# A fused attention, soft-MoE and feed-forward kernel on one core: the combine softmax divided between the routing tail and the output stage, and the weight conversions cut into finer steps

## The chip, the cores and the metric

The kernel runs on 1 core of one Trainium2 chip. The metric is device time in microseconds; lower is better. In the text PE is TensorE, DVE is VectorE, ACT is ScalarE, POOL is GpSimd and SP is SyncE, which here only issues DMAs. Each engine works through a queue of its own, in order, and waits on semaphores for the others.

## The reference

Three layers follow each other. All inputs are float32.

```python
# attention, q k v: (8, 8, 576, 64), causal in blocks of 64
scores = scale * q @ k.T ; scores[block_i < block_j] = -1e9
x = softmax(scores) @ v                      # reshaped to (4608, 512)
# soft mixture of experts: 8 experts with 4 slots each
logits = x @ phi                             # (4608, 32)
d = exp(logits - logits.max(0)); d /= d.sum(0) + 1e-9      # over the tokens
slot_input = (d.T @ x).reshape(8, 4, 512)
slot_out[e] = relu(slot_input[e] @ w1[e]) @ w2[e]          # 512 -> 1024 -> 512
c = exp(logits - logits.max(1)); c /= c.sum(1) + 1e-9      # over the slots: combine
x = c @ slot_out.reshape(32, 512)
# feed forward, 512 -> 2048 -> 512
r = relu(x @ w_in); g = s * (r * r) + b
out = g @ w_out
```

## The kernel before

**Attention and routing** (0 to 433 us). 32 pairs of heads pass through a hand-written schedule: the table `SLOT` gives each step an offset, `at` puts it into `plan`, and `run` issues all steps sorted by time. The order of code here is the order in every engine's queue. After each fourth pair one batch is routed: its tokens are transposed and copied (xT), multiplied by phi (L469, L482), the running maximum `nrun` over tokens is updated (L473, L485), the exponentials are transposed (d, L509) and the weighted sum of tokens is added to `acc` (route_x, L511 to L527). `route_n` copies the logits to `lgs` (L532). After the last batch `route_w` (L540 to L544) makes W4, the weights that bring the four groups of partial sums together.

**Weights.** w1 and w2 of the experts come in 32 loads of 1 MB (w1 and w2, index 0 to 15 each), every load being two DMAs of 512 KB (load_w, L101). The 8 `wi` and 8 `wo` loads of the feed-forward layer hold 64-bit words, which are turned into float32 on chip by `from_f64`: two passes on DVE (cve L619, cvm L620), two on ACT (L622, L623), two on DVE (cvf L625, cve L626). Then a `wi` gets one multiplication (L739). A `wo` gets a multiplication (value, L702), a sum of absolute values and from it a power of two (power: ACT L706, DVE L709, ACT L711) and is split into two float16 halves (high: ACT L719, low: DVE L724). `from_f64` is a generator: a `yield` ends a step, and `convert` advances every active conversion by one step. Twelve loads come in during attention. The rest need a place: NPOST places of 1 MB, freed by `used` when an expert is done with its weights, and half of the place pairs of `wi` and `wo` that are through with conversion. SP issues all loads in a fixed order (advance, L684).

**The tail of routing** (L594 to L604). Thirteen `convert` calls are put into the plan, 0.8 of a schedule unit apart, so conversions of wi_0 to wi_3 go between the steps of the last batch's routing.

**The expert stage.** slotT, the slots' inputs, is made (L777, L778). Then `expert1` runs over the 16 w1 loads, all adding into one PSUM tile hp; `mid` (L828) evicts hp (hs), transposes it and applies relu (hTz); `expert2` runs over the 16 w2 loads into so. After each expert one `convert` follows, with at most two conversions active. Six generators `combine` (groups of six token tiles each) do the combine softmax and take a free slot among the active conversions: maximum (DVE), subtraction (POOL), exponential (ACT), sum and reciprocal (DVE), product (POOL), and the split into two float16 halves (ACT, POOL).

**The slots stage.** so is evicted (sos, L890), transposed, and multiplied by the eight converted `wi`; the result is scaled into mst (L887 to L939).

**The output stage.** 12 groups of three token tiles by 16 blocks of the hidden dimension give 192 steps: h (PE, L982), r (ACT, L984), g (DVE, L990), rh (ACT, L996), rl (DVE, L998), and nine matmuls into three output tiles (L1010 to L1012), which are issued LAG = 4 steps later. `ctrans` transposes the combine weights of the next group halfway through each.

Of the kernel before, what the change touches and what calls it, by code (L numbers as in the profile page):

```python
# [8 lines left out]
F32 = mybir.dt.float32  # L9
F32R = mybir.dt.float32r  # L10
F16 = mybir.dt.float16
# [3 lines left out]
AF = mybir.ActivationFunctionType  # L15
# [2 lines left out]
PSUM = bass.MemoryType.PSUM  # L18

NPRE = 12  # L20
NPOST = 4

SLOT = {
    "ld_k": -28.8, "ld_q": -28.6, "ld_v": -18.0,
# [8 lines left out]
}  # L33

# [6 lines left out]
def fused_kernel(  # L41
# [218 lines left out]
    def lo(eng, o, i, h):  # L260
        eng = {"P": POOL, "D": DVE}.get(eng, eng)
        eng.tensor_tensor(out=o, in0=i, in1=h, op=ALU.subtract)  # L262
# [285 lines left out]
    def at(tau, pri, fn, *args):  # L548
        plan.setdefault(tau, []).append((pri, len(plan[tau]) if tau in plan else 0, fn, args))
# [61 lines left out]
    def from_f64(w, pool, finish):  # L611

        v = w.rearrange("p (n t) -> p n t", t=2)
        l32, h32 = v[:, :, 0].bitcast(U32), v[:, :, 1]
        n = w.shape[1] // 2
        m = pool.tile([128, n], I32, tag="cvm", name="cvm", bufs=1)
        e = pool.tile([128, n], I32, tag="cve", name="cve")
        f = pool.tile([128, n], F32, tag="cvf", name="cvf")
        DVE.tensor_scalar(out=e, in0=h32, scalar1=1, scalar2=21, op0=ALU.logical_shift_left, op1=ALU.logical_shift_right)  # L619
        DVE.tensor_scalar(out=m, in0=h32, scalar1=0xFFFFF, scalar2=None, op0=ALU.bitwise_and)  # L620

        ACT.activation(out=f, in_=l32, func=AF.Copy, scale=2.0 ** -52, bias=1.0)  # L622
        ACT.activation(out=e, in_=e, func=AF.Relu, bias=m896, scale=2.0 ** 23)  # L623
        yield
        DVE.scalar_tensor_tensor(out=f, in0=m, scalar=2.0 ** -20, in1=f, op0=ALU.mult, op1=ALU.add)  # L625
        DVE.scalar_tensor_tensor(out=e, in0=h32, scalar=-0x80000000, in1=e, op0=ALU.bitwise_and, op1=ALU.bitwise_or)  # L626
        for fn in finish:
            fn(f, e.bitcast(F32))
            yield
# [22 lines left out]
    def later(stack, name, bufs, side="left"):  # L652
        return stack.enter_context(tc.tile_pool(name=name, bufs=bufs, side=side, reuse_waits="tile"))

    P = {}
    wlate = wholes(ctx, "wlate", 16 - NPRE, reuse_waits="tile")
    e1 = later(ctx, "e1", 1)
    P["cv"] = later(ph2, "cv", 2)
    wpost = places(ph2, "wpost", NPOST, reuse_waits="tile")
    ready, todo, active = set(), [], []  # L660
# [36 lines left out]
    def split_wo(i):  # L697
# [6 lines left out]
        def power(u, s):  # L704
            for h in range(2):
                ACT.activation(out=s[:, 512 * h:512 * h + 512], in_=u[:, 512 * h:512 * h + 512], func=AF.Abs, bias=eps,  # L706
                               accum_out=wsum[:, 2 * i + h:2 * i + h + 1])

            DVE.tensor_scalar(out=wpow[:, 2 * i:2 * i + 2].bitcast(I32), in0=wsum[:, 2 * i:2 * i + 2].bitcast(I32),  # L709
                              scalar1=0x7F800000, scalar2=0x7F800000, op0=ALU.bitwise_and, op1=ALU.bitwise_xor)  # L710
            ACT.mul(wpow[:, 2 * i:2 * i + 2], wpow[:, 2 * i:2 * i + 2], 2.0 ** 13)  # L711
# [17 lines left out]
                empty.append(split(home["wo", i], i))  # L729
                advance()  # L730

        return from_f64(wt["wo", i], P["cv"], [value, power, high, low])

    def conv_in(i):

# [11 lines left out]
    def convert(most):  # L747

        pump(active)
        if todo and len(active) < most and todo[0] in wt:  # L750
            key = todo.pop(0)
            active.append((conv_in if key[0] == "wi" else split_wo)(key[1]))

    T = dict(pe=1, g=0.447, r=1.648)

    CSUB = 1
    CMOST = 2
    with tc.manual_schedule():
        advance()
    todo += [key for key in wseq if key[0] in ("wi", "wo")]  # L760
    for i in range(13):
        at(TEND + 0.8 * i, 20, convert, 1)
    run(TEND, 1000)
    rt.close()
    P["cs"] = later(ctx, "csp", 1, "right").tile([128, NT, 64], F16, name="cs")
    e2 = later(ctx, "e2", 2, "right")
    P["hTz"] = later(ph2, "hp2", 1, "right").tile([128, 8, 288], F32, name="hTz")
    POOL.memset(P["hTz"], 0.0)
    pa = ph2.enter_context(tc.tile_pool(name="pa", bufs=1, space=PSUM, reuse_waits="tile"))
    pb = ph2.enter_context(tc.tile_pool(name="pb", bufs=2, space=PSUM, reuse_waits="tile"))  # L770
    with tc.manual_schedule():
# [11 lines left out]
        hp = pa.tile([128, 512], F32, name="hp")  # L783
        so = pa.tile([128, 512], F32, name="so")
        hs = e1.tile([128, 512], F32, tag="a1", name="hs")

        def combine(T, n):

            lg = lgs[:, T:T + n, :]
            mc = e2.tile([128, 6, 1], F32, tag="mc", name="mc")  # L790
            DVE.tensor_reduce(out=mc[:, :, 0], in_=lg, axis=AX, op=ALU.max)
            c = e2.tile([128, 6, 32], F32, tag="c", name="c")
            POOL.tensor_tensor(out=c, in0=lg, in1=mc.to_broadcast([128, n, 32]), op=ALU.subtract)
            yield
            ACT.activation(out=c, in_=c, func=AF.Exp)
            yield
            sc = e2.tile([128, 6, 1], F32, tag="sc", name="sc")
            DVE.tensor_reduce(out=sc[:, :, 0], in_=c, axis=AX, op=ALU.add)
            DVE.tensor_scalar(out=sc, in0=sc, scalar1=1e-9, scalar2=2.0 ** -14, op0=ALU.add, op1=ALU.mult)
            DVE.reciprocal(out=sc, in_=sc)  # L800
            yield
            POOL.tensor_tensor(out=c, in0=c, in1=sc.to_broadcast([128, n, 32]), op=ALU.mult)
            o = P["cs"][:, T:T + n, :]
            hi(ACT, o[:, :, 0:32], c)
            lo(POOL, o[:, :, 32:64], c, o[:, :, 0:32])

        done = {"w1": 0, "w2": 0}

# [35 lines left out]
                          start=(done["w2"] == 0), stop=(done["w2"] == 15))  # L844
            done["w2"] += 1

        combs = [combine(6 * i, 6) for i in range(6)]
        for kind, i in [x for x in wseq if x[0] in ("w1", "w2")]:
            if kind == "w2" and done["w2"] == 0:
                mid()  # L850
            (expert1 if kind == "w1" else expert2)(i)
            used((kind, i))
            if done["w1"] == 4 and kind == "w1":
                sums()
            for _ in range(CSUB):
                convert(CMOST)
            if combs and done["w1"] >= 4 and len(active) < CMOST:
                active.append(combs.pop(0))
        while todo or active or combs:
            convert(CMOST)  # L860
            if combs and len(active) < CMOST:
                active.append(combs.pop(0))
    ph2.close()


# [110 lines left out]
    with tc.manual_schedule():  # L976
# [51 lines left out]
        def at(t, fn, *args):  # L1028
            ops_at.append((t, len(ops_at), fn, args))

        for n, (g, f) in enumerate(seq):
            if f == 8 and g + 1 < NG:
                at(n - .1, ctrans, g + 1, ps_h, "h")
            at(n, stage_h, g, f)
            at(n + T["g"], stage_g, g, f)
            at(n + T["r"], stage_r, g, f)
            at(n + LAG + .05, stage_o, g, f)
            if f == 15:
                at(n + LAG + .06, stage_e, g)
# [31 lines left out]
```

## Time and profile before

| | |
|---|---|
| runs, us | 997.34, 994.86, 996.08 |
| median of the runs, us | 996.08 |
| profiled execution, us | 995.35 |
| its span, us | 993.6 |
| attention and routing up to the last normalisation | 0 to 433 us |
| tail of routing, up to the first expert matmul | to 463 us |
| expert stage, up to the eviction of so | to 553 us |
| slots stage, up to the first output matmul | to 578 us |
| output stage | to 993.6 us |
| busy over the span | PE 869.9, DVE 702.0, ACT 604.2, POOL 284.2 us |
| mean granted TensorE clock | 0.95 |

The span is the time from the first to the last instruction on the core; the execution's own time is 1.75 us longer. Busy shares are means over stages that have different limits, so a change in one stage is read from the rows of that stage: which wait ends last in it. Starts in a timeline are us from the start of the span; a row that merges several instructions says so with its count.

### The profile page before, as it was taken

Reading aid. Unit: us, or ns where it says so; the run is one execution under the profiler, and the core shown is the slowest. Engines: PE = TensorE matmul, PEld = TensorE weight load, DVE = VectorE, ACT = ScalarE, POOL = GpSimd, SP = SyncE. Lnnn points to the kernel's source line nnn. Section 1 sums busy time; section 2 is a strip of 40 time slices with the busy share of each in tenths; the row PEclk is TensorE's granted clock in tenths of the full one; section 3 lists DMA queues with packets and bytes.
Section 4 is the critical chain, followed back from the end, with each engine's and each line's share of the span. In section 5 each row is a group of like instructions: output and inputs, shape, how many; then the busy total and the mean of one; then the engine's idle time right before and its main releaser. Section 6 shows DMA issues by size and latency. Waiting matters only on the chain.

```text
span 993.6 us, 20491 instructions
## 1 busy us (share of the span) xinstructions
PE 869.9 (88%) x8052; PEld 517.7 (52%) x8052; DVE 702.0 (71%) x1269; ACT 604.2 (61%) x1040; POOL 284.2 (29%) x224
## 2 busy tenths in 40 slices
PE   3899989988999899955827689999999999999998
PEld 2677767767777777741111334444444444444443
DVE  5798979878989889858877565555555555555553
ACT  2677767767777767753466655555555555555553
POOL 6576747655666657630000300000000000000000
PEclk9999999989999999975859779999999999999999
DMA  5534445344444443084987000001000100010001
GB/s 113 130 88 121 123 106 124 79 118 113 108 90 121 123 107 96 17 337 173 392 339 280 1 1 32 1 33 33 32 1 32 32 1 32 33 32 1 33 32 32
DMA packets 150927, 91.73 MB, mean 92 GB/s; under 512 B 127472, under 2 KB 127792, under 8 KB 150832
## 3 DMA queue, kind: packets, MB, share of 16 engines
q1 hardware_dynamic: 150832, 90.44, 30.4%
q8 instruction: 63, 1.03, 0.4%
q14 instruction: 32, 0.26, 0.1%
HBM read 80.81 MB, written 9.44 MB: 91 GB/s over the span
## 4 chain that ended last, share of the span: by engine, by line
PE 57%; DVE 25%; ACT 10%; issue 3%; POOL 3%; DMA 2%; SPq 1%; DVEq 0%; POOLq 0%; ACTq 0%
PE o L1011 13%; PE o L1012 13%; PE o L1010 13%; DVE vl L356 5%; PE s L378 5%; DVE mm L292 3%; ACT pc L383 3%; PE h L982 3%; PE tp L268 2%; ACT ph L255 2%; DVE cvf L625 2%; DVE cve L626 2%; PE s L303 2%; PE pv L416 1%; DVE me L292 1%
## 5 line engine op out<-in xcount | busy, mean ns | idle before, releaser
L262 POOL TENSOR_TENSOR pl<-pc,ph 128x896 f16<-128x896 f32 (+1 forms) x128 | 232.7, 1819 | 150.4 <-ACT ph L255 75.9
L990 DVE SCALAR_TENSOR_TENSOR g<-r,sk 128x384 f32<-128x384 f32 x192 | 118.5, 617 | 137.9 <-ACT r L984 136.5
L984 ACT ACTIVATE r<-h,msum 128x384 f32<-128x384 f32 x192 | 111.4, 581 | 160.4 <-PE h L982 159.2
L383 ACT ACTIVATE pc<-s 128x896 f32<-128x896 f32 (+1 forms) x128 | 110.7, 865 | 76.9 <-PE s L378 48.4
L998 DVE SCALAR_TENSOR_TENSOR rl<-g,bk,rh 128x384 f16<-128x384 f32 x192 | 117.5, 612 | 6.7 <-ACT rh L996 6.7
L996 ACT ACTIVATE rh<-g,bk 128x384 f16<-128x384 f32 x192 | 116.3, 606 | 2.2 <-DVE g L990 2.2
L255 ACT CAST ph<-pc 128x896 f16<-128x896 f32 (+1 forms) x128 | 113.4, 886 | 4.1
L292 DVE TENSOR_REDUCE mm<-s 128x2 f32<-128x1024 f32 (+3 forms) x128 | 101.9, 818 | 7.9 <-PE s L303 7.6
L416 PE MATMUL pv<-vh,ph 128*128 128x65 f16 x960 | 102.4, 196 | 1.1 <-DVE xt L432 1.0
L418 PE MATMUL pv<-vh,pl 128*128 128x65 f16 x960 | 100.8, 194 | 1.3 <-POOL pl L262 1.3
L417 PE MATMUL pv<-vl,ph 128*128 128x64 f16 x960 | 101.1, 193 | 0.0
L416 PEld LDWEIGHTS <-ph 128*128 128x128 f16 x960 | 86.5, 98 | 23.0 <-issue 6.5
L1012 PEld LDWEIGHTS <-rl 128*128 128x128 f16 x576 | 56.5, 98 | 69.0 <-issue 0.8
L1010 PEld LDWEIGHTS <-rh 128*128 128x128 f16 x576 | 56.6, 98 | 66.9 <-issue 0.8
L418 PEld LDWEIGHTS <-pl 128*128 128x128 f16 x960 | 88.5, 98 | 1.6 <-POOL pl L262 1.5
L417 PEld LDWEIGHTS <-ph 128*128 128x128 f16 x960 | 88.5, 99 | 0.0
L1011 PEld LDWEIGHTS <-rh 128*128 128x128 f16 x576 | 56.6, 98 | 58.6 <-issue 1.1
L262 DVE TENSOR_TENSOR kql<-tp,kq 128x512 fp32r<-128x512 f32 (+1 forms) x96 | 57.5, 600 | 28.9 <-ACT kq L284 27.9
L268 PE MATMUL tp<-idF,rqk 128*128 128x128 f32 x320 | 57.8, 298 | 21.9 <-DVE kql L262 9.5
L303 PE MATMUL s<-kq 64*128 64x64 f32 (+4 forms) x384 | 55.5, 337 | 20.2 <-DVE me L292 13.7
L378 PE MATMUL s<-mr,neg 64*128 64x128 f32 (+3 forms) x384 | 66.6, 318 | 5.7 <-DMA mr<-mT 5.5
L378 PE MATMUL s<-kq 64*128 64x128 f32 (+3 forms) x384 | 70.8, 365 | 0.7
(236 smaller groups left out, 1897.1 us busy)
## 6 DMA issues: line engine op xcount, KB each, us to landing
w<-in_moe_w_dram SPq DMA_DIRECT2D x32, 512.0 KB
w2h<-in_moe_w_dram SPq DMA_DIRECT2D x32, 512.0 KB
rqk<-in_k_dram SPq DMA_DIRECT2D x64, 128.0 KB
rqk<-in_q_dram SPq DMA_DIRECT2D x64, 128.0 KB
rv<-in_v_dram SPq DMA_DIRECT2D x64, 128.0 KB
wi<-in_moe_w_in_dram SPq DMA_DIRECT2D x8, 1024.0 KB
wo<-in_moe_w_out_dram SPq DMA_DIRECT2D x8, 1024.0 KB
out_dram<-ob SPq DMA_DIRECT2D x32, 256.0 KB
```

The lines of the kernel that those rows point to most:

```text
L255: ACT.copy(o, i)
L262: eng.tensor_tensor(out=o, in0=i, in1=h, op=ALU.subtract)
L292: DVE.tensor_reduce(out=o, in_=i, axis=AX, op=ALU.max)
L378: PE.matmul(ps[:, h, o:o + c1 - c0], a[r], b[r], start=(n == 0), stop=(n == 3))
L383: ACT.activation(out=pc[:, :, 0:w], in_=st.pop(("ps", p, c))[:, :, 0:w], func=AF.Exp, scale=scale)
L416: PE.matmul(o, a, vh[:, 2 * sl + h, 0:65], start=(c == 0 and n == 0), stop=False)
L417: PE.matmul(o[:, 0:64], a, vl[:, 2 * sl + h, :], start=False, stop=False)
L418: PE.matmul(o, l, vh[:, 2 * sl + h, 0:65], start=False, stop=(c == 3 and n == len(UNIT[c]) - 1))
L990: DVE.scalar_tensor_tensor(out=g0, in0=r, scalar=sk[:, f:f + 1], in1=r, op0=ALU.mult, op1=ALU.mult)
L1010: PE.matmul(o, rh[:, 128 * i:128 * i + 128], hl[f][0], start=(f == 0), stop=False)
L1011: PE.matmul(o, rh[:, 128 * i:128 * i + 128], hl[f][1], start=False, stop=False)
L1012: PE.matmul(o, rl[:, 128 * i:128 * i + 128], hl[f][0], start=False, stop=(f == 15))
```

## The change

The change has four parts.

- **Routing tail.** `convert` is called seven times at chosen points in place of thirteen, so wi_0 and the beginning of wi_1 lie there. `route_w` is planned earlier (`rw` from 7.316 to 1.299), ahead of d and acc. The first of the six combine groups is advanced five times there.
- **Combine.** `combine` becomes a function ahead of the tail. The other five groups are no longer advanced in the expert stage but in the output stage: group i has four steps, at 16(2i − 1) − 5 + 2j + 0.3 for j = 0 to 3.
- **Finer steps.** Two `yield`s are added in `from_f64`, and `power` is divided into `power` (ACT) and `power2` (DVE L709 before, ACT L711 before).
- **Places.** NPOST goes from 4 to 3, and one place `wright` opens on the right side of memory after the routing's tiles are released. The tiles of the combine (cs, e2) are allocated earlier, on the left.

```diff
-NPOST = 4
+NPOST = 3
...
-    "route": 13.708, "re": 1.322, "tt0": -8.174, "rp": -0.708, "rw": 7.316, "tt": -0.734, "tl": 0.899, "rt": 12.9,
+    "route": 13.708, "re": 1.322, "tt0": -8.174, "rp": -0.708, "rw": -0.2 + 0.899 + 0.6, "tt": -0.734, "tl": 0.899, "rt": 12.9,
...
         DVE.scalar_tensor_tensor(out=f, in0=m, scalar=2.0 ** -20, in1=f, op0=ALU.mult, op1=ALU.add)
+        yield
         DVE.scalar_tensor_tensor(out=e, in0=h32, scalar=-0x80000000, in1=e, op0=ALU.bitwise_and, op1=ALU.bitwise_or)
+        yield
         for fn in finish:
...
+    P["cs"] = later(ctx, "csp", 1).tile([128, NT, 64], F16, name="cs")
+    e2 = later(ctx, "e2", 2)
...
+        def power2(u, s):
             DVE.tensor_scalar(out=wpow[:, 2 * i:2 * i + 2].bitcast(I32), in0=wsum[:, 2 * i:2 * i + 2].bitcast(I32),
...
-        return from_f64(wt["wo", i], P["cv"], [value, power, high, low])
+        return from_f64(wt["wo", i], P["cv"], [value, power, power2, high, low])
...
-    CSUB = 1
...
-    for i in range(13):
-        at(TEND + 0.8 * i, 20, convert, 1)
+    z = 8 * (NP - 1) + O["route"]
+    for t in (O["rp"] - 0.01, O["rp"] - 0.005, O["tl"] + 0.1, O["re"] + 0.3, O["re"] + 0.35, O["rx"] + 0.2, O["rx"] + 0.3):
+        at(z + t, 7, convert, 1)
+    combs = [combine(6 * i, 6) for i in range(6)]
+    for i in range(5):
+        at(z + O["rx"] + 0.5 + i, 20, pump, [combs[0]])
     run(TEND, 1000)
     rt.close()
-    P["cs"] = later(ctx, "csp", 1, "right").tile([128, NT, 64], F16, name="cs")
-    e2 = later(ctx, "e2", 2, "right")
     P["hTz"] = later(ph2, "hp2", 1, "right").tile([128, 8, 288], F32, name="hTz")
     POOL.memset(P["hTz"], 0.0)
+    empty += places(ph2, "wright", 1, side="right", reuse_waits="tile")
+    with tc.manual_schedule():
+        advance()
...
-            for _ in range(CSUB):
-                convert(CMOST)
-            if combs and done["w1"] >= 4 and len(active) < CMOST:
-                active.append(combs.pop(0))
-        while todo or active or combs:
             convert(CMOST)
-            if combs and len(active) < CMOST:
-                active.append(combs.pop(0))
+        while todo or active:
+            convert(CMOST)
...
+        def step(gen):
+            next(gen, None)
+
+        for i in range(1, 6):
+            for j in range(4):
+                at(16 * (2 * i - 1) - 5 + 2 * j + 0.3, step, combs[i])
```

**Order, place one: DVE in the tail of the routing**, from the last normalised tokens (xt) on. cve, cvm, cvf are the passes of a 64-bit conversion, wi_627 is wi_0; mb, mt and nrun are the maxima. Before:

```order
L432 TENSOR_TENSOR xt<-pv,rr 64x128
L619 TENSOR_SCALAR cve<-wi_627 128x1024
L620 TENSOR_SCALAR cvm<-wi_627 128x1024
L625 SCALAR_TENSOR_TENSOR cvf<-cvm,cvf 128x1024
L626 SCALAR_TENSOR_TENSOR cve<-wi_627,cve 128x1024
L739 TENSOR_TENSOR wi_627<-cvf,cve 128x1024
L251 COPY xT<-tp 128x512
L251 COPY xTt<-tp 128x128
L292 TENSOR_REDUCE mb<-tp 128x1
L473 SCALAR_TENSOR_TENSOR nrun_111<-mb,nrun_110 128x1
```

And now:

```order
L432 TENSOR_TENSOR xt<-pv,rr 64x128
L251 COPY xT<-tp 128x512
L251 COPY xTt<-tp 128x128
L619 TENSOR_SCALAR cve<-wi_627 128x1024
L620 TENSOR_SCALAR cvm<-wi_627 128x1024
L292 TENSOR_REDUCE mb<-tp 128x1
L473 SCALAR_TENSOR_TENSOR nrun_111<-mb,nrun_110 128x1
L292 TENSOR_REDUCE mt<-s 32x1
L485 SCALAR_TENSOR_TENSOR nrun_111<-mt,nrun_111 32x1
L625 SCALAR_TENSOR_TENSOR cvf<-cvm,cvf 128x1024
L540 TENSOR_REDUCE W_112<-s 128x32
L541 TENSOR_SCALAR W_112<-W_112,nrun_111 128x32
```

wi_0's five passes stood ahead of xT; now xT and xTt come first, two passes of wi_0 fill the time up to mb, one the time behind nrun, and W comes directly behind it. The combine's mc and sc come further down this queue, ahead of lgs and slotT.

**Order, place two: ACT in the middle of the expert stage**, around the eviction of layer one (hs) and its relu (hTz). wo_5777 and wo_6396 are wo_0 and wo_1, wo_2s holds the split halves of wo_2 and wo_3. Before:

```order
L711 ACTIVATE wpow<-wpow 128x2
L719 ACTIVATE wo_2s<-cvf,wpow 128x512 x2
L706 ACTIVATE cve,wsum<-cvf,eps 128x512 x2
L711 ACTIVATE wpow<-wpow 128x2
L829 ACTIVATE hs<-hp,rs 128x512
L834 ACTIVATE hTz<-htp 128x32x4 x2
L719 ACTIVATE wo_2s<-cvf,wpow 128x512 x2
L622 ACTIVATE cvf<-wo_8666 128x1024
```

And now:

```order
L622 ACTIVATE cvf<-wi_5120 128x1024
L623 ACTIVATE cve<-cve,m_103 128x1024
L839 ACTIVATE hs<-hp,rs 128x512
L844 ACTIVATE hTz<-htp 128x32x4 x2
L622 ACTIVATE cvf<-wo_5777 128x1024
L623 ACTIVATE cve<-cve,m_103 128x1024
L622 ACTIVATE cvf<-wo_6396 128x1024
L623 ACTIVATE cve<-cve,m_103 128x1024
```

hs and hTz stood among the split of wo_3; now they stand between the last `wi` and wo_0.

**Order, place three: DVE at the end of the conversions**, from the last block's third pass on; wo_6s holds the split halves of wo_6 and wo_7. Before:

```order
L709 TENSOR_SCALAR wpow<-wsum 128x2
L625 SCALAR_TENSOR_TENSOR cvf<-cvm,cvf 128x1024
L626 SCALAR_TENSOR_TENSOR cve<-wo_8672,cve 128x1024
L702 TENSOR_TENSOR cvf<-cvf,cve 128x1024
L709 TENSOR_SCALAR wpow<-wsum 128x2
L724 SCALAR_TENSOR_TENSOR wo_6s<-cvf,wpow,wo_6s 128x512 x4
L791 TENSOR_REDUCE mc<-lgs 128x6 x2
L798 TENSOR_REDUCE sc<-c 128x6
```

And now:

```order
L715 TENSOR_SCALAR wpow<-wsum 128x2
L627 SCALAR_TENSOR_TENSOR cve<-wo_8673,cve 128x1024
L706 TENSOR_TENSOR cvf<-cvf,cve 128x1024
L730 SCALAR_TENSOR_TENSOR wo_6s<-cvf,wpow,wo_6s 128x512 x2
L898 COPY soT<-m 128x128
L715 TENSOR_SCALAR wpow<-wsum 128x2
L642 COPY ct<-n 64x384
L730 SCALAR_TENSOR_TENSOR wo_6s<-cvf,wpow,wo_6s 128x512 x2
L909 COPY part<-m 128x256
```

The four `low` stood together behind the last wpow and ahead of two combine groups (mc); now two stand ahead of that wpow, two behind it, soT and ct of the slots stage come between, and no combine follows.

## Rows read from the trace of the kernel before

**Rows 1.** Windows: stretch and length; busy us and count of each engine; PEclk, DMA share, GB/s.

```profile
434.80:463.20 28.40, 11.99 (x69) 6.97 (x68) 23.86 (x39) 10.06 (x14) 2.02 (x1) 0.56 0.58 219
...
583.60:986.00 402.40, 402.40 (x1925) 186.14 (x1923) 225.91 (x397) 220.65 (x407) 0.00 (x0) 1.00 0.06 22
```

**Rows 2.** Timeline of the routing tail: start, duration, engine, line, operation, [idle before <-releaser].

```profile
435.44 0.42 PE L268 MATMUL tp<-idF,xt 128*128 128x128 f32 x1
...
439.83 0.69 DVE L251 COPY xT<-tp 128x512 f32<-128x512 f32 x1
...
444.50 0.15 DVE L485 SCALAR_TENSOR_TENSOR nrun<-mt,nrun 32x1 f32<-32x1 f32 x1
...
448.14 0.32 DVE L509 COPY d<-s 128x160 f32<-128x160 f32 x1
...
452.13 0.80 PE L538 MATMUL s<-idF,nrun 128*128 128x128 f32 x2
...
452.26 2.02 POOL L768 MEMSET hTz<- 128x2304 f32 x1 [19.80 <-PE s L518]
...
453.30 0.74 DVE L520 SCALAR_TENSOR_TENSOR acc<-acc,f,s 128x512 f32<-128x512 f32 x1
...
454.71 0.15 DVE L527 TENSOR_TENSOR ssum<-ssum,st 32x1 f32<-32x1 f32 x1
...
459.71 0.28 DVE L540 TENSOR_REDUCE W<-s 128x32 f32<-128x128 f32 x1
...
460.91 1.88 PE L777 MATMUL stp<-W,acc 128*128 128x32 f32 x8 [6.09 <-DVE W L543]
...
463.25 1.08 PE L815 MATMUL hp<-w,slotT 128*32 128x512 f32 x4 [0.45 <-DVE slotT L778]
```

**Rows 3.** Timeline: weight stream in layer one, and the first wo pass on DVE.

```profile
465.22 0.33 SPq L111 DMA_DIRECT2D w<-in_moe_w_dram  x1
...
481.22 1.04 PE L815 MATMUL hp<-w,slotT 128*32 128x512 f32 x2
...
483.99 0.69 DVE L619 TENSOR_SCALAR cve<-wo 128x1024 int32<-128x1024 int32 x1
...
495.34 1.06 PE L815 MATMUL hp<-w,slotT 128*32 128x512 f32 x6 [0.23 <-DMA w<-in_moe_w_dram]
```

**Rows 4.** Timeline of the middle of the expert stage.

```profile
514.07 0.67 ACT L829 ACTIVATE hs<-hp,rs 128x512 f32<-128x512 f32 x1
...
517.19 1.33 ACT L719 ACTIVATE wo_2s<-cvf,wpow 128x512 f16<-128x512 f32 x2
...
517.94 1.42 DVE L724 SCALAR_TENSOR_TENSOR wo_2s<-cvf,wpow,wo_2s 128x512 f16<-128x512 f32 x2 [2.71 <-ACT wo_2s L719]
...
518.41 1.15 ACT L622 ACTIVATE cvf<-wo 128x1024 f32<-128x1024 uint32 x1
...
519.27 0.68 DVE L619 TENSOR_SCALAR cve<-wo 128x1024 int32<-128x1024 int32 x1
```

**Rows 5.** Waits from 485.3 to 552 us: total us, times, longest.

```profile
DVE wpow L709 <- ACT cve L706: 14.4, 8, 2.0
```

**Rows 6.** Timeline from the last wo block to the first output matmul.

```profile
546.24 1.22 DVE L702 TENSOR_TENSOR cvf<-cvf,cve 128x1024 f32<-128x1024 f32 x1
...
551.77 0.61 DVE L791 TENSOR_REDUCE mc<-lgs 128x6 f32<-128x192 f32 x2
...
552.20 0.98 POOL L793 TENSOR_TENSOR c<-lgs,mc 128x192 f32<-128x192 f32 x2 [97.92 <-DVE mc L791]
...
553.48 0.57 ACT L890 COPY sos<-so 128x512 f32<-128x512 f32 x1
...
553.73 0.19 DVE L800 RECIPROCAL sc<-sc 128x6 f32<-128x6 f32 x1
...
578.11 0.50 PE L982 MATMUL h<-ct,mst 128*128 128x384 f16 x1 [1.92 <-DVE mst L939]
```

**Rows 7.** The page's costliest groups: xcount | busy, mean ns | idle before, releaser.

```profile
L990 DVE SCALAR_TENSOR_TENSOR g<-r,sk 128x384 f32<-128x384 f32 x192 | 118.5, 617 | 137.9 <-ACT r L984 136.5
```

More of the change, by code (lines that the diff above doesn't have):

```diff
@@ L752, in convert, with combine @@
             active.append((conv_in if key[0] == "wi" else split_wo)(key[1]))
+    def combine(T, n):
+        lg = lgs[:, T:T + n, :]
+        mc = e2.tile([128, 6, 1], F32, tag="mc", name="mc")
+        DVE.tensor_reduce(out=mc[:, :, 0], in_=lg, axis=AX, op=ALU.max)
+        c = e2.tile([128, 6, 32], F32, tag="c", name="c")
+        POOL.tensor_tensor(out=c, in0=lg, in1=mc.to_broadcast([128, n, 32]), op=ALU.subtract)
+        yield
+        ACT.activation(out=c, in_=c, func=AF.Exp)
+        yield
+        sc = e2.tile([128, 6, 1], F32, tag="sc", name="sc")
+        DVE.tensor_reduce(out=sc[:, :, 0], in_=c, axis=AX, op=ALU.add)
+        DVE.tensor_scalar(out=sc, in0=sc, scalar1=1e-9, scalar2=2.0 ** -14, op0=ALU.add, op1=ALU.mult)
+        DVE.reciprocal(out=sc, in_=sc)
+        yield
+        POOL.tensor_tensor(out=c, in0=c, in1=sc.to_broadcast([128, n, 32]), op=ALU.mult)
+        o = P["cs"][:, T:T + n, :]
+        hi(ACT, o[:, :, 0:32], c)
+        lo(POOL, o[:, :, 32:64], c, o[:, :, 0:32])
     T = dict(pe=1, g=0.447, r=1.648)
-    CSUB = 1
     CMOST = 2
@@ L785, in fused_kernel @@
         hs = e1.tile([128, 512], F32, tag="a1", name="hs")
[L787 to L805, printed above, removed]
         done = {"w1": 0, "w2": 0}
@@ L845, in expert2 @@
             done["w2"] += 1
-        combs = [combine(6 * i, 6) for i in range(6)]
         for kind, i in [x for x in wseq if x[0] in ("w1", "w2")]:
```

## The prediction

> **What bounds the kernel now.** I read the windows first. In the output stage TensorE is busy for all 402.4 us and VectorE (DVE) for 225.9 of them, so that stage is TensorE's, and nothing but fewer matmuls shortens it. The two stretches ahead of it are not: in the routing tail DVE has 23.9 us of work in 28.4 while TensorE has 12.0 [rows 1]. So I read the timeline of the tail row by row, then that of the weight stream and of the middle of the expert stage, then the waits of the `wo` conversions, then the timeline into the slots stage, and last the page's row of the output stage.
>
> The tail shows DVE working in the wrong order for the chain. TensorE's last transposes of the batch end at 435.86 (435.44 + 0.42), but DVE copies them (xT) only at 439.83, since wi_0's five conversion passes stand ahead in its queue. The same happens in front of d (448.14), acc (453.30) and W (459.71); the first expert matmul starts at 463.25 [rows 2].
>
> Behind it the weights stream: the load issued at 465.22 begins 20 half-loads of 512 KB that arrive one by one until 495.34, which is when TensorE can finish layer one [rows 3]. ScalarE (ACT) evicts that layer only at 514.07, because eviction stands in its queue behind the conversion of four `wo` blocks, so it holds nothing up except one `high` (517.19) and the DVE `low` behind it, 2.71 us late [rows 4]. What ends last here is the DVE–ACT chain of the `wo` conversions: it decides when the second layer's result is evicted (sos, 553.48), and from sos the slots stage takes 24.6 us to the first output matmul at 578.11 [rows 6]. In these conversions DVE waits eight times for ACT's abs, 14.4 us in all [rows 5].
>
> **The change, step by step.** The profiled execution took 995.35 us against a span of 993.6, and the median of the runs is 0.7 us above it, so I move its span and add 2.5 us at the end. Everything up to 433.2 is the same.
>
> *Tail.* Now xT is ahead of wi_0: about 435.75, not 439.83. The last nrun ended 4.82 us after xT began (444.65) with two conversion passes in between, and they are again two, so 440.5. TensorE's matmul on nrun takes 0.80, the W steps 1.2 (459.71 until TensorE used W at 460.91), so d starts at 442.75. From d to the end of TensorE's routing sums was 4.1 us (448.14 to 452.26), which gives acc at 446.85, and ssum 1.56 later (453.30 to 454.86), 448.4. Only the finish of wi_0 and two passes of wi_1 remain on the way [rows 2].
> The new thing in this queue is a combine group. Its first POOL operation stands behind the memset of hTz, 2.02 us, which waits for ssum, so POOL starts at 450.5. From the first POOL operation of a group to its reciprocal was 1.72 us (552.20 to 553.92), so DVE stands until 452.25 and only then copies lgs and slotT: first expert matmul about 452.85. Without the combine it would be 449.9, so the combine costs 3 us here [rows 2, 6]. The gain so far is 10.4 us.
>
> *Weight stream.* NPOST goes from 4 to 3 and one place opens on the right once the routing's tiles are gone, so places stay four and this price is nothing as long as a place comes back in time. The old stream had w1_4 and w1_5 loaded before the first expert ran, since conversions had freed their places; the new one has not. So at 454.85 (465.22 − 10.4, first place freed) 24 halves are to come, not 20. Between the 9th (481.22) and the 20th (495.34) a half took 1.284 us, and 465.22 to 481.22 leaves 4.4 us beside nine of these. 454.85 + 4.4 + 24 × 1.284 = 490.1, and TensorE ends layer one 1.06 later, 491.2 [rows 3].
> [...]
>
> *The middle.* The order puts hs and hTz directly behind the last `wi` pass on ACT and ahead of wo_0. That is a new wait: DVE's cvf of wo_0 needs ACT's first pass, which now needs hp. Behind that ACT instruction all eight `wo` are queued. hs at 491.2, next ACT work 3.12 us later as before (514.07 to 517.19), the pass 1.15: DVE's cvf of wo_0 at 495.5 [rows 4]. DVE itself is ready sooner: four `wi` conversions and the small sums took 20.7 us (463.25 to 483.99), 6.7 of them take 34.7, so DVE comes to wo_0 near 487.6 and to cvf 1.3 later; it stands for about 6 to 7 us [rows 2, 3]. The old 2.71 us stall is gone in exchange.
>
> *The split conversions.* A pair of `wo` took 16.25 us (519.27 to 551.77, two pairs), of which 3.6 were waits for abs (14.4 over four pairs); 12.65 is work [rows 4 to 6]. Now the two `low` of the first block (1.4 us) stand between a value and the next wpow, where DVE waited up to 2.0 us, and the next block's first two passes stand ahead of the second block's `low`. I leave 0.6 of wait at each of the two places: 13.9 per pair. Three periods gain 7.1, the first pair 1.1 by its one wait for abs.
>
> *The end of the expert stage.* sos came 1.7 us behind the last pair because two combine groups stood ahead of it, and the pair itself had ended with wo_7's abs, wpow and four `low`, 4.3 us from its value (546.24 + 1.22 = 547.46) to 551.77 [rows 6]. In the new order of ACT sos comes after wo_6's `high` and ahead of wo_7's abs. That `high` depends on a wpow which stands two DVE passes (2.45 us) before wo_7's value is finished, and with ACT's scaling and its two passes of 1.33 together it ends 0.75 us before that value does. wo_0's first pass began at 483.99 and two passes of 0.69 brought cvf to 485.4 [rows 3]; from there to sos (553.48) was 68.1; now 68.1 − 2.7 − 7.1 − 1.1 − 1.7 − 4.3 − 0.75 = 50.45. So sos is at 495.5 + 50.45 = 545.95, 7.5 us sooner. The second layer's matmuls (56 halves from 454.85) are not in the way: 454.85 + 4.4 + 56 × 1.284 = 531.2.
>
> *Slots and output.* wo_7's abs and `high` (3.4 us of ACT) and four `low` (2.9 us of DVE) move into the slots stage, and four combine groups go out of it. As they are of like size, I book 0.6 us of gain, with bounds of −1 to +2. In the output stage five groups are added, 20 steps over 144 of 192 outputs. 1925 matmuls at 10.2 a step are 189 steps, so a step takes TensorE 2.13 us, while DVE has two passes of about 0.62 of its own in it; a group brings DVE one pass of 0.3 (551.77) and three no longer (553.73), an estimate of 1.0 in two pieces [rows 6]. The outputs run four steps behind (LAG), so a late piece is caught up: I take zero, bounded by one step for each group, 5 × 2.13 = 10.7 us [rows 1, 7].
>
> **Sum.** 7.5 + 0.6 = 8.1 us: span 985.5, execution 987.25, median 988. The changes in the tail and in the stream carry little of this by themselves (of the 10.4 us, four more halves take 5.1, and a new stall takes the place of an old one); the pairs and the end carry most.
>
> **Rivals.** (a) *The new wait in the middle is shorter.* If the halves land at the rate of a freer stream, or ACT comes to hs only after hp is done, up to 7 us of stall go: 981. For it: the stream's 4.4 us offset is read once. Against: the rate of 1.284 held over 11 halves. Chance 0.10.
> (b) *The combine groups aren't hidden in the output stage.* POOL does nothing there now [rows 1], so no row shows a POOL operation beside DVE's g and rl. If each of 15 POOL operations (0.49 us, from [rows 6]) holds up a DVE one and the chain r, g, rh, rl has no slack, 15 × 0.49 = 7.4 us comes back: 995.4, no change. Against: DVE idles 44% there, and LAG is four steps. Chance 0.07.
> [...]
> (c) *Slower: the stream is bound by places.* With three old places and the one on the right, a place must come back within 8 × 1.284 = 10.3 us of its load's issue; it now takes about 4.4 + 2.5 us. If it takes longer, each half costs more, hp is later one for one, and all eight `wo` behind it. The 24 halves turn the gain over at 1.284 + 8.1/24 = 1.62 us each; at 1.9 us they cost 24 × 0.62 = 14.8 and the time is about 1003. For it: w1_7 and w1_13 wait for places that conversions give back on DVE, the queue that now is late. Against: by the count above wi_1 and wi_3 are through when asked. Chance 0.05.
> (d) *The pairs keep their waits.* If ACT's order lets the same 3.6 us stand, 3 × 2.4 us are lost: 995, no change. Chance 0.05.
>
> **Numbers.** The forecast has 0.73, the rivals 0.27. About 0.3%, 3.0 us, is what a measurement of this kernel can tell from no change. Faster by more than that (below 993.1): the forecast, (a) and a little of (b) and (d) where they hold in part, 0.84; within: the rest of (b) and (d), 0.10; slower: (c) and the bound of 10.7 in the output stage on top of a smaller gain, 0.06. The range goes down to (a), 981, and up by the bounds of the slots stage (1.6), of the 0.6 us waits left in each pair (a doubling of them costs 3.6) and of the handovers in the tail (0.8), which won't all come together: 993.5. It leaves out (b), (c) and (d), 0.17 in all.
>
> **What would show it.** xT at 435.8 and the first expert matmul near 453, with POOL's hTz ahead of c; hs at once behind hp near 491, and DVE's cvf of wo_0 waiting for ACT some 6 us; a pair period of 13.9; sos near 546 and the first output matmul near 570; TensorE busy throughout the output stage. A layer one that ends after 495, a TensorE gap at the output steps 11 to 17 or 43 to 49, or sos after wo_7's `high` would prove a step wrong.

## The result and the profile after

The changed kernel takes 983.13 us (median of four runs, 981.15 to 985.49) against 996.66 for the kernel before (994.86 to 997.34, four runs): ratio 0.9868, 95% interval 0.9842 to 0.9894. That is 13.5 us faster; 8.1 had been forecast, with a range of 981.0 to 993.5.

The profiled execution took 982.77 us, its span 981.1. First the tail, from the timeline (start, duration, engine, line, operation, idle before and releaser), with the rows that answer to [rows 2]:

```profile
434.61 0.42 PE L268 MATMUL tp<-idF,xt 128*128 128x128 f32 x1
434.86 0.69 DVE L251 COPY xT<-tp 128x512 f32<-128x512 f32 x1 [0.95 <-PE tp L268]
...
439.58 0.15 DVE L485 SCALAR_TENSOR_TENSOR nrun<-mt,nrun 32x1 f32<-32x1 f32 x1
...
442.08 0.32 DVE L509 COPY d<-s 128x160 f32<-128x160 f32 x1
...
446.61 0.15 DVE L527 TENSOR_TENSOR ssum<-ssum,st 32x1 f32<-32x1 f32 x1
446.69 0.68 DVE L619 TENSOR_SCALAR cve<-wi 128x1024 int32<-128x1024 int32 x1
446.90 3.02 POOL L795 MEMSET hTz<- 128x2304 f32 x1 [15.27 <-DVE ssum L527]
447.29 0.67 DVE L620 TENSOR_SCALAR cvm<-wi 128x1024 int32<-128x1024 int32 x1
...
450.82 0.35 DVE L771 TENSOR_REDUCE sc<-c 128x6 f32<-128x192 f32 x1 [2.59 <-ACT c L768]
...
451.72 0.28 DVE L808 COPY slotT<-stp 128x128 f32<-128x128 f32 x1
...
452.05 6.11 PE L825 MATMUL hp<-w,slotT 128*32 128x512 f32 x32 [4.14 <-DVE slotT L808]
```

xT now waits for TensorE and not for wi_0. Near the end DVE stands 2.59 us for the combine group, because POOL's memset of hTz is ahead of it. The first expert matmul starts at 452.05 (before, 463.25).

The weight stream, the middle and the end of the expert stage, in place of [rows 3], [rows 4] and [rows 6]:

```profile
454.03 4.13 SPq L111 DMA_DIRECT2D w<-in_moe_w_dram  x6
...
458.87 1.06 PE L825 MATMUL hp<-w,slotT 128*32 128x512 f32 x8
...
460.41 1.04 PE L825 MATMUL hp<-w,slotT 128*32 128x512 f32 x2 [0.47 <-DMA w<-in_moe_w_dram]
...
488.52 1.06 PE L825 MATMUL hp<-w,slotT 128*32 128x512 f32 x6 [0.27 <-DMA w<-in_moe_w_dram]
489.67 0.69 ACT L839 ACTIVATE hs<-hp,rs 128x512 f32<-128x512 f32 x1 [7.08 <-PE hp L825]
490.41 1.10 PE L842 MATMUL htp<-I,hs 128*128 128x64 f32 x8 [0.82 <-ACT hs L839]
...
491.94 1.19 ACT L622 ACTIVATE cvf<-wo 128x1024 f32<-128x1024 uint32 x1
...
493.16 1.23 DVE L625 SCALAR_TENSOR_TENSOR cvf<-cvm,cvf 128x1024 f32<-128x1024 int32 x1 [6.35 <-ACT cvf L622]
...
518.06 0.69 DVE L619 TENSOR_SCALAR cve<-wo 128x1024 int32<-128x1024 int32 x1
...
531.92 0.69 DVE L619 TENSOR_SCALAR cve<-wo 128x1024 int32<-128x1024 int32 x1
...
542.84 1.23 DVE L706 TENSOR_TENSOR cvf<-cvf,cve 128x1024 f32<-128x1024 f32 x1
543.19 0.56 ACT L894 COPY sos<-so 128x512 f32<-128x512 f32 x1
...
567.04 0.50 PE L986 MATMUL h<-ct,mst 128*128 128x384 f16 x1 [1.92 <-DVE mst L943]
```

ACT waits 7.08 us for layer one and DVE 6.35 us for ACT: the new wait is there. A pair of `wo` takes 13.86 us (518.06 to 531.92), and sos follows 0.35 us behind the start of wo_7's value, where it was 7.2 us behind. The waits of 480 to 560 us (total, times, longest) show where [rows 5] went; the abs wait of 14.4 us is down to 3.5:

```profile
ACT hs L839 <- PE hp L825: 7.1, 1, 7.1
DVE cvf L625 <- ACT cvf L622: 6.7, 3, 6.3
...
DVE wpow L715 <- ACT cve L710: 3.5, 7, 0.7
```

In the kernel before, the transposes of hs took longer:

```profile
514.79 1.97 PE L832 MATMUL htp<-I,hs 128*128 128x64 f32 x8 [18.39 <-ACT hs L829]
```

For every kernel below I split the profiled span at the same four rows: xt (the last normalised tokens), the start of wo_7's value, sos, and the first h that needs the second part of mst (567.04 above; it is what the prediction calls the first output matmul, though the very first h starts 4.1 us ahead of it, at 562.91 here and at 573.98 before). xt lies in code that is the same everywhere, yet it came between 433.6 and 437.4 us in these profiles, so stages are compared from xt on.

| kernel | median, us (runs) | xt to value of wo_7 | to sos | to h | to the end |
|---|---|---|---|---|---|
| before | 996.66 | 111.8 | 7.2 | 24.6 | 415.5 |
| changed | 983.13 (981.15 to 985.49) | 109.2 | 0.35 | 23.85 | 414.0 |
| e1 coarse steps | 993.68 (992.88 to 996.71) | 114.7 | 4.5 | 23.8 | 415.7 |
| e2 combine in expert stage | 987.42 (985.81 to 987.85) | 109.3 | 0.35 | 26.1 | 414.2 |
| e3 group 0 later | 980.08 (975.85 to 982.03) | 104.2 | 0.35 | 24.1 | 414.1 |
| e4 first wo ahead of hs | 983.58 (982.32 to 985.71) | 104.5 | 4.5 | 23.6 | 415.5 |
| e5 = e4, sos kept early | 980.40 (979.15 to 981.20) | 104.4 | 0.35 | 24.4 | 414.4 |
| e6 old tail | 989.44 (987.93 to 989.82) | 108.7 | 4.5 | 23.6 | 415.5 |
| e7 fine steps alone | 990.82 (988.72 to 993.44) | 106.8 | 4.7 | 28.5 | 415.4 |
| e8 = e5 and e3 | 977.11 (976.11 to 979.68) | 101.6 | 0.35 | 24.3 | 414.3 |
| e9 output groups twice | 985.56 (984.18 to 986.81) | 108.7 | 0.35 | 24.1 | 414.1 |
| e10 three places | 987.61 (986.20 to 989.98) | 111.5 | 0.35 | 24.3 | 414.2 |
| e11 = e6, sos kept early | 984.90 (983.80 to 985.05) | 108.1 | 0.35 | 24.5 | 414.4 |
| e12 sos last | 988.55 (987.00 to 989.56) | 109.8 | 4.5 | 24.9 | 414.6 |

The kernel before was measured again beside each group of runs. Its medians lie between 995.27 and 996.66 us, and the ratios below are to the median of the same group.

From xt to the end the change took 559.1 down to 547.4, 11.7 us: 2.6 before the value of wo_7, 6.9 between it and sos, 0.8 in the slots stage, 1.5 in the output stage. The 1.5 us lie where the output stage begins at half clock. One window each (columns as in [rows 1]) holds the rise of TensorE's granted clock from 0.50 to 1.00. Before:

```profile
583.00:584.00 1.00, 1.00 (x4) 0.40 (x3) 0.57 (x2) 0.90 (x2) 0.00 (x0) 0.61 0.00 0
```

And now:

```profile
569.50:570.00 0.50, 0.50 (x3) 0.22 (x2) 0.50 (x2) 0.50 (x2) 0.00 (x0) 0.78 0.00 0
```

A mean of 0.61 over the first puts the rise at 583.8, one of 0.78 over the second at 569.7.

### The profile page after: what moved, and what is told of

The parts are those of the page before. It is cut to its first block, busy times and chain, and to the rows that moved or that the text cites. A ratio compares the mean times of both kernels' runs of the same rounds, so it can differ in the third digit from the quotient of the medians.

```text
span 981.1 us, 20487 instructions
## 1 busy us (share of the span) xinstructions
PE 879.0 (90%) x8052; PEld 515.1 (53%) x8052; DVE 703.6 (72%) x1269; ACT 604.1 (62%) x1040; POOL 286.5 (29%) x224
## 4 chain that ended last, share of the span: by engine, by line
PE 58%; DVE 21%; ACT 11%; DMA 4%; issue 3%; POOL 3%; SPq 0%; DVEq 0%; POOLq 0%; ACTq 0%
PE o L1015 13%; PE o L1014 13%; PE o L1016 13%; DVE vl L356 5%; PE s L378 4%; DVE mm L292 4%; ACT pc L383 4%; PE h L986 3%; ACT ph L255 3%; PE tp L268 2%; DMA w<-in_moe_w_dram 2%; PE s L303 2%; DVE me L292 2%; PE pv L416 1%; DVE kql L262 1%
## 5 line engine op out<-in xcount | busy, mean ns | idle before, releaser
L766 POOL TENSOR_TENSOR c<-lgs,mc 128x192 f32<-128x192 f32 x6 | 3.0, 508 | 345.6 <-DVE mc L764 345.6
```

## The experiments

**e1, coarse steps in the expert stage.** The tail keeps the fine ones.

```diff
-        yield
+        if fine:
+            yield
...
-            yield
+            if fine or fn.__name__ != "power":
+                yield
...
+    fine = [1]
...
     run(TEND, 1000)
+    fine.clear()
```

> The changed kernel, with the expert stage's conversions in the coarse steps of before (the tail keeps the fine ones, so the tail is the same). Theory (the wo conversions on DVE and ACT set the end of the expert stage): a pair of wo goes back from 13.9 to 16.2 us and sos stands again behind wo_7's abs and high; but with coarse steps eviction of layer one moves behind wo_1 on ACT and the 6.4 us stall of DVE ahead of wo_0 goes. sos 543.2 + 6.5 = about 549.5 to 550, the time about 989.5. Rival (the finer steps matter little, the gain is in the tail and the stream): sos within 2 us of 543.2, the time 983 to 985; if the stall's end were worth its full length and the pairs nothing, 977.

Measured 993.68, ratio to before 0.9984 (0.9972 to 0.9996). Nearly all of the gain is gone, more than forecast: pairs start at 489.79, 506.04, 524.07 and 540.32, that is 16.25, 18.03 and 16.25 us. Layer one is evicted just ahead of the middle one (hs at 504.98), and the first cvf in it waits 1.89 us for ACT's pass behind hTz. Of the 4 us beyond the forecast 1.8 are that (18.03 against 16.25) and 1.7 the output stage (415.7 against 414.0); the rest is not assigned. The finer steps are the part of the change without which the rest is worth about 2 us.

**e7, the finer steps alone**, in the kernel before.

```diff
+        yield
         DVE.scalar_tensor_tensor(out=e, in0=h32, scalar=-0x80000000, in1=e, op0=ALU.bitwise_and, op1=ALU.bitwise_or)
+        yield
...
+        def power2(u, s):
...
-        return from_f64(wt["wo", i], P["cv"], [value, power, high, low])
+        return from_f64(wt["wo", i], P["cv"], [value, power, power2, high, low])
```

> The kernel before, with the finer steps alone (the yields in the 64-bit conversion and the divided power step); tail, places and combine as before. Theory (the finer steps carry most of the gain, as e1 showed from the other side): pair period 13.9 us, cvf of wo_1 behind hTz near 495, sos behind wo_7 and a combine group near 545 to 546, combine groups in the slots stage as before, the time 987 to 990. Rival (they pay only together with the new tail and the moved groups): pair period down, but the time 992 or more.

Measured 990.82, ratio 0.9954 (0.9937 to 0.9970): 4.5 us by itself, a little less than forecast. The pairs have 13.8 us, the value of wo_7 comes 5.0 us earlier after xt, sos 7.5. But the slots stage grows from 24.6 to 28.5 us. Its start, in e7's timeline:

```profile
547.87 0.56 ACT L894 COPY sos<-so 128x512 f32<-128x512 f32 x1
...
551.95 0.55 POOL L262 TENSOR_TENSOR cs<-c,cs 128x192 f16<-128x192 f32 x1 [0.46 <-ACT cs L255]
...
552.55 0.53 PE L639 MATMUL n<-idH,cs 128*64 128x128 f16 x3 [2.14 <-POOL cs L262]
...
553.00 2.79 PE L905 MATMUL m<-wi,soT 128*32 128x256 f32 x24
```

TensorE's transposes of the first combine group stand ahead of the slots' matmuls with `wi`, and they wait 2.14 us for a group that has now less time ahead of sos. The `wi` matmuls start 5.1 us after sos; in the kernel before they started 2.9 us after it (sos at 553.48):

```profile
556.40 1.08 PE L901 MATMUL m<-wi,soT 128*32 128x256 f32 x8
```

So half of what the finer steps gain up to sos comes back in the next stage: 2.2 of the 3.8 us in this wait, the rest is not assigned. With the groups moved (the first into the tail, the others to the output stage) the changed kernel keeps it, and e2 shows what five of them cost in their old place.

**e2, combine groups 1 to 5 back in the expert and slots stage.**

```diff
             convert(CMOST)
-        while todo or active:
+            if len(combs) > 1 and done["w1"] >= 4 and len(active) < CMOST:
+                active.append(combs.pop(1))
+        while todo or active or len(combs) > 1:
...
-        for i in range(1, 6):
-            for j in range(4):
-                at(16 * (2 * i - 1) - 5 + 2 * j + 0.3, step, combs[i])
```

> The changed kernel, with combine groups 1 to 5 not in the output stage but in the expert stage and the slots stage, as before; group 0 stays in the tail. Theory (groups are hidden in the output stage and not hidden ahead of it): sos does not move (543.2, the groups come behind it in the order), but the slots stage, where DVE and ACT work on part and mf, gets 5 groups of about 1.1 us DVE and 0.7 us ACT: first output matmul 1.5 to 5 us later, the time 985 to 988. Rival (the groups cost the output stage something, one TensorE step of 2.1 us or 7.4 us in all): the output stage from first to last output matmul gets shorter by that, and the time is 983 or lower.

Measured 987.42, ratio 0.9922 (0.9904 to 0.9939), as the theory had it: sos stays 0.35 us behind the value, the slots stage takes 26.1 in place of 23.85 us, and the output stage gets no shorter (414.2 against 414.0).

**e9, the output groups twice.**

```diff
         for i in range(1, 6):
+            twin = combine(6 * i, 6)
             for j in range(4):
                 at(16 * (2 * i - 1) - 5 + 2 * j + 0.3, step, combs[i])
+                at(16 * (2 * i - 1) - 5 + 2 * j + 1.3, step, twin)
```

> The changed kernel, with each of the five combine groups of the output stage computed twice, the second time one step later and into the same tiles: ten groups of work on DVE, POOL and ACT where there were five. Theory (they are hidden behind TensorE): TensorE stays busy without a gap, the time from the first to the last output matmul within 0.5 us of the changed kernel's, the time 982.5 to 984. Rival (a POOL operation holds up DVE, and each group costs): if a group costs 7.4/5 = 1.5 us, the time 990; if one TensorE step each, 993.8.

The profile decides here: the output stage takes 414.12 us with ten groups, 414.01 with five, and TensorE has no gap in either. The windows, e9's:

```profile
600.00:900.00 300.00, 300.00 (x1437) 138.81 (x1436) 180.98 (x332) 172.07 (x326) 17.73 (x26) 1.00 0.07 25
```

and the changed kernel's:

```profile
600.00:900.00 300.00, 300.00 (x1437) 138.77 (x1435) 175.62 (x316) 169.63 (x317) 7.04 (x12) 1.00 0.07 24
```

1437 matmuls in either, with DVE 5.4 us and POOL 10.7 us busier. The median, 985.56, lies 1.6 us above the forecast and 2.4 above the changed kernel's, beyond what the stages show (from xt to the end 547.3 against 547.4). Its profiled execution had xt 1.55 us later; what the other runs had is not known.

**e3, the first combine group out of the tail.**

```diff
-    for i in range(5):
-        at(z + O["rx"] + 0.5 + i, 20, pump, [combs[0]])
...
             convert(CMOST)
+            if done["w1"] >= 5 and done["w2"] == 0:
+                next(combs[0], None)
```

> The changed kernel, with the first combine group moved from the tail to the expert stage (one step with each expert from the fifth on), so that slotT no longer waits for POOL's memset and the group. Theory (the combine costs about 3 to 4 us in the tail, and the stream hands it on one for one to eviction, to wo_0 and to the end): first expert matmul near 448 in place of 452.05, layer one's end near 486, DVE's stall ahead of wo_0 down to 3 us or less, the time 980. Rival (DVE's own work up to wo_0 is the limit, or the stream): first expert earlier, but cvf of wo_0 within 1 us of 493.2, the time 982.5 to 984.

Measured 980.08, ratio 0.9841 (0.9813 to 0.9869). From xt, slotT comes 3.8 us earlier (14.3 against 18.1) and the value of wo_7 5.0 us. DVE's stall ahead of wo_0 is 4.05 us, where 3 or less had been forecast. The step in the tail was the one part of the change that cost time.

**e4, wo_0's first passes ahead of hs.**

```diff
             if kind == "w2" and done["w2"] == 0:
+                for _ in range(1):
+                    convert(CMOST)
                 mid()
```

> The changed kernel, with one more conversion step issued ahead of the eviction of layer one, so that ACT's two passes for wo_0 stand ahead of hs. Theory (the stall of 6.4 us at wo_0 is ACT's queue, and DVE is ready): DVE's cvf of wo_0 follows the last wi directly, near 487; DVE then works until wo_1's cvf, which waits for ACT behind hTz, with a rest of stall of 0 to 2 us; sos 4 to 6 us earlier, the time 977 to 979. Rival (the stall only moves to the next place, abs or wpow of wo_0 behind hs): sos within 1.5 us, the time 982 to 983.5.

Measured 983.58, ratio 0.9884 (0.9865 to 0.9903): no gain, but not by the rival's way. The stall of 6.35 us did go, of which 1.17 came back at wo_1's cvf, and the value of wo_7 came 4.8 us sooner after xt. Then sos lost it:

```profile
541.76 1.33 ACT L725 ACTIVATE wo_6s<-cvf,wpow 128x512 f16<-128x512 f32 x2
542.52 1.42 DVE L730 SCALAR_TENSOR_TENSOR wo_6s<-cvf,wpow,wo_6s 128x512 f16<-128x512 f32 x2 [1.02 <-ACT wo_6s L725]
543.00 0.56 ACT L896 COPY sos<-so 128x512 f32<-128x512 f32 x1
```

The 541.76 row is the `high` of wo_7. In the changed kernel sos stood ahead of wo_7's abs, though in the code all conversions come before it; ACT's order comes from the build and not from the code alone, and one more step upstream turned it round.

**e5, e4 with sos fixed in its place.** slot_rows moves into the expert stage, between two steps of the last conversions.

```diff
...
+        rows = slot_rows()
+        left = 5
         while todo or active:
             convert(CMOST)
+            if not todo:
+                left -= 1
+                if left in (0, -1):
+                    next(rows, None)
```

> The kernel of e4 (first wo ahead of the eviction of layer one), with the eviction of the second layer's result (sos) written out between wo_6's high and wo_7's abs on ACT, where the changed kernel has it and e4 lost it. Theory (e4 did shorten the conversions by 4.3 us, and all of it went because sos then stood behind wo_7's abs, scaling and high): sos near 539, the slots stage as long as in the changed kernel, the time 979 to 980. Rival (the slots stage is held by wo_7's own conversion, whenever sos comes): sos near 539, but the first output matmul within 1 us of that of e4, the time 982.5 to 984.

Measured 980.40, ratio 0.9849 (0.9832 to 0.9865), 0.4 above the forecast, with sos at 539.33 and a slots stage of 24.4 us: the theory.

**e12, the other way round**, the changed kernel with sos fixed behind wo_7's `high`.

```diff
...
         while todo or active:
             convert(CMOST)
+        slot_rows()
...
-        slot_rows()
```

> The changed kernel with one thing moved: sos stands behind wo_7's high on ACT, where e4, e6 and e1 had it. Theory: everything up to wo_7's value as in the changed kernel, sos 4.1 us later, TensorE's granted clock rises later in the output stage (1.3 us, as in e4), the time 987.5 to 989. Rival (the slots stage absorbs it because part waits for ACT anyway): the time 983 to 985.

Measured 988.55, ratio 0.9926 (0.9911 to 0.9940), 5.4 us slower than the changed kernel by the medians and 6.3 by the stages from xt. 4.1 are sos itself, 1.0 the slots stage; the output stage gives 0.6 of the 1.3 us expected, and 0.6 come up ahead of wo_7's value, where the edit does nothing. So the place of one eviction in ACT's queue is worth over a third of the whole gain.

**e6, the old tail**, and **e11**, the old tail with sos fixed as in e5.

```diff
-    ... "rw": -0.2 + 0.899 + 0.6, ...
+    ... "rw": 7.316, ...
...
-    for t in (O["rp"] - 0.01, O["rp"] - 0.005, O["tl"] + 0.1, O["re"] + 0.3, O["re"] + 0.35, O["rx"] + 0.2, O["rx"] + 0.3):
-        at(z + t, 7, convert, 1)
+    for i in range(13):
+        at(TEND + 0.8 * i, 20, convert, 1)
```

> The changed kernel, with the routing tail's table of before: 13 conversion steps 0.8 apart (they are fine steps now, so wi_0, wi_1 and the most of wi_2 lie there) and route_w late; all else as changed. Theory (the tail's order sets the first expert, the end of the stream and the stall ahead of wo_0): first expert matmul 5 to 7 us later, layer one's end 2 to 4 us later because conversions have freed places by then, sos as much later, the time 985 to 987. Rival (DVE's total work up to wo_0 is the same in either order, so nothing is gained by it): sos within 1 us, the time 982.5 to 984.

> The kernel of e6 (old tail) with sos written out between wo_6's high and wo_7's abs. Theory (e6 lost its 6 us not in the tail but because sos slid behind wo_7's high): value of wo_7 as in e6 (109 us after xt), sos half a us behind its start, the time 983.5 to 985.5, so the new order of the tail is worth 2 us or less by itself. Rival (the tail decides): the time stays at 987 or more.

e6 took 989.44 (0.9937, 0.9922 to 0.9951), e11 984.90 (0.9887, 0.9871 to 0.9904). With the old tail the first expert starts at 459.23 in e6, 7.0 us later after xt than in the changed kernel, and the value of wo_7 comes at 108.7 and 108.1 us, no later than 109.2. What e6 lost was sos's place, and e11 gets it back. The new tail with the group in it is worth 1.8 us by the medians and nothing by the stages from xt.

**e10, three places.**

```diff
-    empty += places(ph2, "wright", 1, side="right", reuse_waits="tile")
-    with tc.manual_schedule():
-        advance()
```

> The changed kernel without the place on the right: three places for the expert weights, and those that conversions give back. Theory (the stream is bound by the DMA at 1.28 us a half, and four places are enough): with three places a place must come back within 6 x 1.28 = 7.7 us of its issue, and it takes about 7, so the stream stays near 1.28 us a half after the first, which starts one load later (2.6 us): layer one ends 2 to 4 us later, and sos with it, the time 985 to 987. Rival (places decide): a half takes over 1.6 us, layer one ends more than 8 us later, the time 991 or more. If the stream had slack, the time is unchanged, 982.5 to 984.

Measured 987.61, ratio 0.9911 (0.9886 to 0.9936), a little above the forecast. Layer one ends 2.3 us later after xt, sos as much, and by the stages from xt the whole is 2.9 us later, 4.5 by the medians; once under way the stream moves at the same rate (406 to 421 GB/s in e10 from 460 to 488 us, 399 to 421 in the changed kernel). So it loses its start, not its rate, and four places are not short.

**e8, e3 and e5 together**, has their edits and no others.

> The kernel of e5 with e3's edit as well (first combine group out of the tail into the expert stage). Theory (e3 and e5 shorten different links of one chain): sos near 536, the time 976 to 977. Rival (the second layer's weight stream or its matmuls end the stage before that): sos not ahead of 538, the time that of e5.

Measured 977.11 us, ratio 0.9819 (0.9802 to 0.9837): the fastest, 6.0 us below the changed kernel. sos came 102.0 us after xt; in the changed kernel 109.6. It lies at 539.35 and not near 536, since xt was 3.8 us later in the profiled execution.

## Why the prediction was right

The sign, the range and the mechanism held; the size came out 5.4 us short, by several small errors of one sign. Two of them, 1.7 us together, are not known to come from the change, so that part of the gain is luck. By its own steps:

- **Tail.** Forecast 10.4 us sooner to the first expert, measured 11.2, of which 0.83 is xt. One sum in it is off (440.5 + 0.80 + 1.2 is 442.5, not 442.75). The combine in it was forecast at 3 us and costs 3.8 (e3), since the memset took 3.02 us where 2.02 had been taken from [rows 2]. That the tail "carries little by itself" held (e11).
- **Stream.** Layer one was to end at 491.2 and did at 489.6 (488.52 + 1.06); without the earlier xt 0.8 us are left over. The offset of 4.4 us was misread, though: it is not what the first half takes. The 32 matmuls from 452.05 on use the four loads already there, and at 458.87 TensorE uses both halves of the first streamed load, issued at 454.03, without a wait; its first wait for a DMA ends at 460.41, with the third half. The trace's record of DMA completions has the first half in at 457.18, 3.15 us after its issue and 1.9 beyond the 1.28 of one half (3.17 us in the kernel before, 465.22 to 468.39). The other 23 halves, up to 488.52, then took 1.36 us each and not 1.284, with two steps of 1.9 and 2.6 us among them whose cause is open. The 4.4 us covered part of that by luck: with it the last half is 0.7 us too late, with the 1.9 us read here it would have been 1.8 too early.
- **Middle.** The stall was forecast at 6 to 7 us and was 6.35. From hs to ACT's next work it took 2.27 us, not 3.12: the transposes of hs took 1.10 us and not 1.97, in a stretch with a granted clock of 1.00 (480 to 492 us, TensorE busy for 9.2 of 12) against 0.50 in the old one (514 to 516 us, TensorE idle from 500 to 512). A term read from a row at half clock was 0.85 too long.
- **Pairs.** 13.9 forecast, 13.86 measured; e1 and e7 show that the yields make it. Rival (d) is out.
- **End.** sos 0.35 behind the start of wo_7's value, where 0.47 (1.22 − 0.75) had been forecast. The prediction read this place from the order and rightly booked over 5 us for it; e12 prices it at 5.4. It did not see how loosely the place was held (e4, e6).
- **Slots and output.** 23.85 us against a forecast of 24.0. The output stage was taken as unchanged, since nothing but fewer matmuls would shorten it, and got 1.5 us shorter. The row behind this is TensorE's granted clock: it rose from 0.50 to 1.00 at 569.7, 2.7 us behind the h at 567.04, and before at 583.8, 5.7 us behind the one at 578.11. An output step took 4.14 us at a clock of 0.50 (h at 578.11 and 582.25, before) and 2.11 at 1.00 (585.11 and 587.22), so 3.0 us less at half clock is 1.5. Why it rose sooner no run settles; over the other kernels it took from 2.9 to 6.0 us. The four with 5.4 and more (e1, e4, e6, e7) all have sos late, but so has e12, with 3.9.
- **Not forecast:** xt 0.83 us sooner, and 0.9 us between the profiles' difference (12.6) and the medians' (13.5). Neither is known to come from the change: xt alone lies up to 3.8 us apart in these profiles. These two, 0.85 in the middle, 0.8 in the stream, 1.5 in the output stage and some tenths more in the conversions and the slots stage make up the 5.4.
- **Rivals.** (a): no, the wait was 6.35 us, as long as forecast, and the time came near this rival's 981 for the other reasons above. When e4 and e5 take the wait away, wo_7's value comes 4.8 us sooner, not 7. (b): no (e9). (c): no (e10).

Rival (b) had a POOL operation hold up a DVE one. The output stage shows longer DVE rows beside POOL, but only single ones, and nothing in the time: in each of the five groups the g beside POOL's product (0.51 us) took 0.80 or 0.81 us, where the longest g of the kernel before took 0.62, and the mean of all 192 went from 617 to 622 ns. As forecast from the rows of idle time, TensorE does not notice: it is busy for all 405.8 us from 570.2 to 976.

## What to carry to other kernels

Where two engines hand one chain of steps back and forth, cut the steps so that each hand-over has another block's work behind it: here that moved no work and removed most of a 14 us wait. Then look at what the saved time exposes, since the side work that lay in those waits needs a new place, best in a stage bound by another engine (e2, e7, e9). And fix the place of an instruction that ends a stage; where it only happens to stand early, an unrelated edit can cost all that it gains (e4), or over a third of the gain of the whole change (e12).

## What was not expected of the hardware

POOL's memset of hTz takes 2.02 us in [rows 2] and 3.02 in the changed kernel, where DVE's first two conversion passes of a block stand beside it (446.69 and 447.29, rows of the tail above). In e6 a DVE multiplication of two inputs stands beside it and it takes 2.02 again, while the conversion pass that starts in its last part takes twice its 0.69 us:

```profile
449.66 1.21 DVE L745 TENSOR_TENSOR wi<-cvf,cve 128x1024 f32<-128x1024 f32 x1
449.88 2.02 POOL L795 MEMSET hTz<- 128x2304 f32 x1 [18.04 <-DVE ssum L527]
...
451.06 1.38 DVE L619 TENSOR_SCALAR cve<-wi 128x1024 int32<-128x1024 int32 x1
```

So the memset takes 1.00 us more beside the two passes and no more beside the multiplication. Which one is late differs: in the changed kernel a pass is running when the memset starts, both passes keep their length (0.68 and 0.67 us), and the second ends 1.06 us behind that start; in e6 the memset is running, and the pass takes 0.69 us more. Other kernels repeat both: 3.02 us beside the same two passes in e4, e5, e8, e9, e10 and e12, and in e11 2.02 us with a pass of 1.38 us in its last part. What lies behind it no run shows. By these rows it was 1 us of the 3.8 that the first combine group cost in the tail.
